# Attention followed by two expert layers on one core: a load issued by ScalarE, ten unread products, and new costs in the planner

## The chip, the core and the metric

The kernel runs on one core of a Trainium2 chip. Five engines of the core work side by side: TensorE (PE, matrix products, with its weight loads as PEld), VectorE (DVE), ScalarE (ACT), GpSimd (POOL) and SyncE (SP, which here issues the transfers). PE reads from the on-chip memory and writes sums to eight banks; the other engines read the banks and write back. The metric is the device time of one execution in microseconds (us), lower is better.

## The reference, cut to what matters

Three stages follow each other, all in float32 (the weights come as float64).

```
scores = q @ k.T / 8, causal mask, softmax       # 2 batches x 12 heads, 448 x 448, head size 64
x = (softmax @ v) laid out as 896 tokens x 768
h = x @ w_in (768 x 2048);  g = h * clip(h + 3, 0, 6) / 6;  y = g @ w_out (2048 x 768)
h = y @ w_in2;  g = P(h) / (Q(h) + 1e-6), P of degree 3, Q of degree 2;  out = g @ w_out2
```

The coefficients of P and Q come from two small arrays `a` (4 numbers) and `b` (2 numbers).

## The kernel before, in words

Every product is made to full accuracy from three products of a number's two parts (a rounded part "hi" and the rest): hi x hi, hi x rest, rest x hi.

**Attention** works on twelve pairs (two heads of one batch). For a pair, `q` and `k` are loaded by two transfers each (`qk_load`, line 340), split into hi and rest (`a_split`, line 355, and `a_rest`, line 360; for pairs 0 and 1 on ACT and DVE, later on POOL), and PE makes four row blocks of scores (`a_scores`, line 364, 24 products; the two heads sit in the two halves of PE's rows). DVE adds the mask and takes the maximum (`a_max`, line 378), ACT takes the exponential (`a_exp`, line 391), PE transposes (`a_transpose`, line 435 of the profile) into banks that ACT or DVE empties (`a_move`), and PE applies the result to `v` (`a_apply`, line 458; the two heads sit in the two halves of PE's columns). The sums of the exponentials are inverted, spread, transposed (`a_turn`, line 415) and multiplied in; `xh` and `xl` are the two parts of the result.

**The expert layers** are 2304 products of 128 x 128 weights with 448 columns (`product`, line 690). Weights come in 128 chunks of three tiles: a load (`w_load`, line 580, tile `raw`), three ACT steps (lines 592, 586, 309) and three DVE steps (596, 602, 620) turn a float64 chunk into two float32 parts. 32 chunks of the third weight stage and what follows it are made early, in the time of the first two stages: they are stored to memory (`w_keep`, line 626) and fetched when they are needed (`w_fetch`, line 630).

**The order** is written by a planner (`Program.order`, line 60). Each operation has an engine or a choice of engines, a cost, what it reads and writes, the buffers that it takes, and a due time (a place in the plan plus the number of its kind in the table `DUE`). The planner takes, again and again, the operation that can begin first by its own clock, and of those that can begin at the same time the one that is due first. What it writes down is the order on each engine; on the chip each engine runs its own list from the top and waits at each instruction for what that one needs. A load counts as 0.655 us on the queue engine (`c_dma`), and 2.2 us pass until another engine may use it. The small arrays are read by `c_load` (lines 562 and 563), turned by DVE into `cneg` (line 566) and by ACT into `cabs` (line 569).

Of the kernel before, what the change touches and what calls it, by code (L numbers as in the profile page):

```python
# [16 lines left out]
P = 128  # L17
CP = 112
NCH = 4
KC = 3  # L20
NA = 3
EARLY = 2, 3
LATE = 16
# [9 lines left out]
class Program:  # L33
# [13 lines left out]
    }  # L47
    BANKS = 8

    def __init__(self, rings, banks, due):  # L50
# [9 lines left out]
    def order(self):  # L60
        ops = self.ops
# [30 lines left out]
        def earliest(n):  # L92
            t = {}
            for e in ops[n][2]:
                t[e] = max((end[b] + self.DELAY[where[b]][e] for b in needs[n]), default=0.0)
            return t

        can = {n: earliest(n) for n in range(n_ops) if not missing[n]}
        due = [op[1] + self.due[op[0]] for op in ops]
        result = []  # L100
        while can:
            best = None
            for n, t in can.items():
# [17 lines left out]
                if room >= 1e9:  # L121
                    continue
                for e, cost in ops[n][2].items():
                    mine = max(t[e], free[e], room), due[n], n, e, cost
                    if best is None or mine < best:
                        best = mine
            if best is None:
                raise RuntimeError("no room")
            begin, _, n, e, cost = best
            start[n], end[n], where[n] = begin, begin + cost, e  # L130
            free[e] = end[n]
# [53 lines left out]
def c_dma(n):  # L185
    return n / 350e3


def c_mm(n, passes):
    return passes * n * 0.000461  # L190

# [75 lines left out]
def tile_attention_moe_moe2(  # L267
# [61 lines left out]
    def a_masks(e):  # L329
# [6 lines left out]
        )  # L336

    add("constants", -50, {"pool": 1.3}, a_masks, writes=["masks"])

    def qk_load(e, which, n):  # L340
# [133 lines left out]
    for n in range(len(pairs)):  # L474
        t = PAIR * n
        for which in ("kr", "qr"):
            raw, hl = (which, n), (SPLIT[which], n)
            add(
                "load", t, {"dma": c_dma(P * 4 * S)}, qk_load, which, n, writes=[raw],
                new=[(which, raw)],  # L480
# [11 lines left out]
        for s, (j, i) in enumerate(order):  # L492
            w = (i + 1) * CP
            if j == 0:
                sc = [("sc", n, h, i) for h in range(2)]
                add(
                    "scores", t + s, {"pe": 0.02 + c_pe(max(w, 224), 3)}, a_scores, n, i,
                    reads=[("kk", n), ("qs", n)], writes=sc, new=[("s", key) for key in sc],
                )
# [323 lines left out]
    def add_products(i, j, batches):  # L823
# [3 lines left out]
        s = [("sum", which, m, b) for b in batches]  # L827
        x = [("g", which, k, b) if which % 2 else ("x", k, b) for b in batches]
        add(
# [14 lines left out]
    for n, c in enumerate(early):  # L844
        add_chunk(c, base + 10 + (whole - 15) * n / len(early), early)
    while i < len(chunks):
# [75 lines left out]
```

## Time and profile before

| | |
|---|---|
| median of three runs | 575.91 us (575.46 to 578.22) |
| the profiled execution | 576.56 us |
| its span, first to last instruction of the program | 574.8 us |
| PE busy | 561.2 us, 98% |
| DVE busy | 440.3 us, 77% |
| ACT busy | 410.8 us, 71% |
| POOL busy | 43.8 us, 8% |
| bytes moved | 87.11 MB |

PE's products overlap and their ends are modelled, so a PE that reads as busy can still be slow or waiting; where it matters, the mean time of one instruction of a given shape and the idle time in brackets tell more than the share.

### The profile page before, as it was taken

The numbers are of one execution on the slowest core, as the hardware profiler recorded it, in microseconds if no ns is written. First come the engines' busy times: TensorE is split into PE (matmuls) and PEld (weight loads), VectorE is DVE, ScalarE is ACT, GpSimd is POOL, SyncE is SP. The second block draws the span as 40 slices with busy tenths as digits, with TensorE's granted clock in tenths as the row PEclk, the third lists the DMA queues.
The fourth block names the chain that finished last, engine by engine and source line by source line (L and its number), as shares of the span: only waits on it lengthen the run. The fifth ranks groups of instructions, "written<-read, shape, count | busy, mean of one in ns | idle before, by whom it ended". The sixth has DMA issues, their size and how long they took to land.

```text
span 574.8 us, 9134 instructions
## 1 busy us (share of the span) xinstructions
PE 561.2 (98%) x3072; PEld 496.3 (86%) x3072; DVE 440.3 (77%) x953; ACT 410.8 (71%) x925; POOL 43.8 (8%) x57
## 2 busy tenths in 40 slices
PE   5999999999999999999999999989999999999997
PEld 4666777899999999999999999979989989999996
DVE  5488888699999999876776449988988988975520
ACT  5499999797978888776676349867767767855420
POOL 3456421100000000000000000000000000000000
PEclk9999999999999999999999999999999999999999
DMA  5854112377677776776667342143322422425200
GB/s 161 233 137 123 34 33 74 105 238 261 220 235 245 227 270 230 253 259 219 217 219 247 111 137 85 56 137 114 134 84 87 160 83 83 137 89 175 87 33 32
DMA packets 35087, 87.11 MB, mean 152 GB/s; under 512 B 4512, under 2 KB 9120, under 8 KB 35040
## 3 DMA queue, kind: packets, MB, share of 16 engines
q1 hardware_dynamic: 35040, 86.53, 46.7%
q8 instruction: 24, 0.39, 0.3%
q14 instruction: 23, 0.19, 0.1%
HBM read 71.18 MB, written 15.34 MB: 151 GB/s over the span
## 4 chain that ended last, share of the span: by engine, by line
PE 73%; DVE 12%; ACT 7%; DMA 3%; issue 2%; SPq 1%; ACTq 0%
PE bank L690 60%; PE bank L435 4%; PE bank L458 4%; PE bank L373 4%; DVE p L767 2%; DVE qy L763 2%; DVE p L765 2%; DMA w<-kept 2%; ACT qy L753 1%; ACT p L735 1%; ACT qy L729 1%; DMA cb<-in_b 1%; DVE p L742 1%; DVE p L739 1%; SPq L346 1%
## 5 line engine op out<-in xcount | busy, mean ns | idle before, releaser
L690 PE MATMUL bank<-yh,w 128*128 128x448 f32 x384 | 113.3, 365 | 0.0
L690 PE MATMUL bank<-rh,w 128*128 128x448 f32 x384 | 98.7, 367 | 2.1 <-DMA w<-kept 2.0
L690 PE MATMUL bank<-xh,w 128*128 128x448 f32 x384 | 95.4, 367 | 0.0
L690 PE MATMUL bank<-ph,w 128*128 128x448 f32 x384 | 93.6, 365 | 0.0
L620 DVE TENSOR_TENSOR w<-full,w 128x384 fp32r<-128x384 f32 x96 | 53.2, 555 | 49.8 <-ACT w L309 48.8
L592 ACT ACTIVATE tail<-raw 128x384 uint32<-128x384 uint8 x128 | 70.4, 558 | 27.3 <-DVE full L596 18.0
L586 ACT ACTIVATE full<-raw 128x384 f32<-128x384 f32 x128 | 69.2, 551 | 26.1 <-DVE w L620 24.6
L596 DVE SCALAR_TENSOR_TENSOR full<-full,tail 128x384 uint32<-128x384 uint32 x128 | 70.3, 556 | 21.0 <-ACT full L586 20.3
L690 PEld LDWEIGHTS bank<-rh,w 128*128 128x128 f32 x384 | 71.7, 188 | 9.2 <-ACT qy L760 2.0
L690 PEld LDWEIGHTS bank<-yh,w 128*128 128x128 f32 x384 | 72.1, 188 | 6.0 <-DVE p L742 0.3
L690 PEld LDWEIGHTS bank<-ph,w 128*128 128x128 f32 x384 | 72.1, 188 | 5.7
L690 PEld LDWEIGHTS bank<-xh,w 128*128 128x128 f32 x384 | 71.5, 188 | 5.5
L309 ACT ACTIVATE w<-full 128x384 fp32r<-128x384 f32 x96 | 50.0, 521 | 36.4 <-PE bank L690 36.2
L690 PE MATMUL bank<-yl,w 128*128 128x448 f32 x192 | 70.1, 365 | 0.0
L602 DVE SCALAR_TENSOR_TENSOR full<-raw,full 128x384 uint32<-128x384 uint32 x128 | 68.5, 552 | 1.5
L690 PE MATMUL bank<-rl,w 128*128 128x448 f32 x192 | 55.0, 365 | 0.0
L690 PE MATMUL bank<-xl,w 128*128 128x448 f32 x192 | 54.5, 365 | 0.0
L690 PE MATMUL bank<-pl,w 128*128 128x448 f32 x192 | 54.5, 365 | 0.0
L393 ACT ACTIVATE e<-e,stat 112x448 f32<-112x448 f32 (+3 forms) x96 | 49.4, 520 | 1.2 <-DVE stat L386 1.2
L386 DVE CUSTOM_DVE_ANT_0 e<-bank,mask 112x448 f32<-112x448 f32 (+3 forms) x96 | 38.3, 442 | 7.4 <-PE bank L373 6.9
L373 PE MATMUL bank<-kk,qs 64*112 64x448 f32 (+3 forms) x288 | 33.7, 357 | 6.7 <-ACT qs L309 6.0
L690 PEld LDWEIGHTS bank<-rl,w 128*128 128x128 f32 x192 | 36.1, 188 | 2.9
(66 smaller groups left out, 774.3 us busy)
## 6 DMA issues: line engine op xcount, KB each, us to landing
raw<-in_w SPq DMA_DIRECT2D x128, 384.0 KB, 3.5
kept<-ws SPq DMA_DIRECT2D x32, 384.0 KB, 3.4
w<-kept SPq DMA_DIRECT2D x32, 384.0 KB, 3.5
kr<-in_kT SPq DMA_DIRECT2D x24, 112.0 KB, 2.8
qr<-in_qT SPq DMA_DIRECT2D x24, 112.0 KB, 2.6
v<-in_v SPq DMA_DIRECT2D x12, 224.0 KB, 2.7
out_T<-o SPq DMA_DIRECT2D x12, 224.0 KB, 3.1
ca<-in_a SPq DMA_DIRECT2D x1, 2.0 KB, 5.2
```

What stands on the lines that cost most here:

```text
L309: e.activation(out, in_, AF.Copy)
L373: e.matmul(tiles["sc", n, j, i], q[rows, qp, i * CP:w], k[rows, kp, :w], start=m == 0, stop=m == 2,)
L386: e.tensor_tensor_reduce(t[:, :w], tiles.pop(("sc", n, j, i)), mask[:, S - w:], -0.125, 3.0e38, ALU.add, ALU.min, tiles["stat", n][:, j, 0 ...
L393: e.activation(t, t, AF.Exp, bias=stat[:, j, 0, i:i + 1], scale=-1.0, accum_out=stat[:, j, 1, i:i + 1],)
L435: e.transpose(pt[:, col:col + CP], tiles["e", n, j, i][:, c * CP:(c + 1) * CP], ident)
L458: e.matmul(o[j * D:(j + 1) * D, c * CP:S], v[:, c, j * D:(j + 1) * D], segs[c, j], start=a == 0, stop=a == 2,)
L586: e.activation(full[i], high, AF.Copy, scale=TO_F32)
L592: e.activation(tail[i], top, AF.Copy, bias=-31.0 / 64.0, scale=1.0 / 32.0)
L596: e.scalar_tensor_tensor(bits, bits, 3, tail.pop(i), ALU.logical_shift_left, ALU.bitwise_or)
L602: e.scalar_tensor_tensor(bits, raw.pop(i)[:, :, :, 1], 0x80000000, bits, ALU.bitwise_and, ALU.bitwise_or)
L620: e.tensor_tensor(split[i][:, 1], full.pop(i), split[i][:, 0], ALU.subtract)
L690: e.matmul(sums[which, m, b], split[i][:, w, j, :], x, start=k == 0 and n == 0, stop=last and n == 2,)
```

## The change

Five edits. (1) The load of pair 0's `q` is given to ACT's queue instead of SP's; every `q` and `k` load counts as 1.26 us, and the delay behind a load is that of a transfer whichever engine issues it. (2) Ten products of the identity with itself, read by nobody, are put on PE ahead of the first scores; they need only the identity that POOL writes. (3) The planner knows three layouts of PE (rows split for scores, columns split for apply, whole for the rest): an operation that would change the layout counts as due 1.0 later, and a change costs PE 0.12. (4) The first products of the expert layers wait until the last pair's scores are made; a product counts as 0.000453 us a column in place of 0.000461. (5) The early chunks start 30 us later in the plan and end at the same place.

```diff
+WARM = 10
+    TILING = {"scores": "rows", "apply": "columns"}
+    DRAIN = 0.12
+    STAY = 1.0
-                t[e] = max((end[b] + self.DELAY[where[b]][e] for b in needs[n]), default=0.0)
+                t[e] = max((
+                    end[b] + self.DELAY["dma" if ops[b][0] == "load" else where[b]][e]
+                    for b in needs[n]
+                ), default=0.0)
+                turn = "pe" in t and self.TILING.get(ops[n][0], "") != tiling
                 for e, cost in ops[n][2].items():
-                    mine = max(t[e], free[e], room), due[n], n, e, cost
+                    mine = max(t[e], free[e], room), due[n] + self.STAY * turn, n, e, cost
+            if e == "pe" and self.TILING.get(ops[n][0], "") != tiling:
+                tiling = self.TILING.get(ops[n][0], "")
+                begin = max(begin, free[e] + self.DRAIN)
-    return passes * n * 0.000461
+    return passes * n * 0.000453
+    def a_warm(e, banks):
+        for _ in range(WARM):
+            e.matmul(bank[banks[0]][:CP, :CP], ident, ident, start=True, stop=True)
+    add(
+        "constants", -49, {"pe": 0.4 * WARM}, a_warm, reads=["masks"], writes=["warm"],
+        new=[("o", "warm")],
+    )
-                "load", t, {"dma": c_dma(P * 4 * S)}, qk_load, which, n, writes=[raw],
+                "load", t, {"act" if n == 0 and which == "qr" else "dma": 1.26}, qk_load, which, n, writes=[raw],
-                    reads=[("kk", n), ("qs", n)], writes=sc, new=[("s", key) for key in sc],
+                    reads=[("kk", n), ("qs", n)], writes=sc + ["scored"] * (n == len(pairs) - 1), new=[("s", key) for key in sc],
-        x = [("g", which, k, b) if which % 2 else ("x", k, b) for b in batches]
+        late = ["scored"] if which == k == 0 else []
+        x = late + [("g", which, k, b) if which % 2 else ("x", k, b) for b in batches]
-        add_chunk(c, base + 10 + (whole - 15) * n / len(early), early)
+        add_chunk(c, base + 40 + (whole - 45) * n / len(early), early)
```

The lists that the planner writes change on every engine. Three places follow. In the names, `kr`, `qr` are the loaded `k`, `q`, `kk`, `qs` their parts, the number behind them is the pair; `e1_03` is the block of pair 1, head 0, row block 3.

**The opening on ACT and DVE.** ACT before:

```order
L305 ACT_TABLE_LOAD
L309 ACTIVATE kk0_116<-kr0_101 128x448
L309 ACTIVATE qs0_122<-qr0_104 128x448
L309 ACTIVATE kk1_127<-kr1_107 128x448
L309 ACTIVATE qs1_133<-qr1_110 128x448
L393 ACTIVATE e0_03_163,stat0_162<-e0_03_163,stat0_162 112x448
```

ACT after:

```order
L318 ACT_TABLE_LOAD
L368 DMA qr0_104<-in_qT 64x448 x2
L322 ACTIVATE kk0_123<-kr0_101 128x448
L322 ACTIVATE kk1_132<-kr1_107 128x448
L322 ACTIVATE qs1_144<-qr1_120 128x448
L415 ACTIVATE e0_03_156,stat0_155<-e0_03_156,stat0_155 112x448
```

DVE before, where L362 makes a rest and L386 the maximum:

```order
L362 TENSOR_TENSOR kk0_116<-kr0_101,kk0_116 128x448
L362 TENSOR_TENSOR qs0_122<-qr0_104,qs0_122 128x448
L362 TENSOR_TENSOR kk1_127<-kr1_107,kk1_127 128x448
L362 TENSOR_TENSOR qs1_133<-qr1_110,qs1_133 128x448
L386 ISA e0_03_163,stat0_162<-bank0_71,mask_88 112x448
```

DVE after (L384 the rest, L408 the maximum):

```order
L324 CAST qs0_125<-qr0_104 128x448
L384 TENSOR_TENSOR qs0_125<-qr0_104,qs0_125 128x448
L384 TENSOR_TENSOR kk0_123<-kr0_101,kk0_123 128x448
L384 TENSOR_TENSOR kk1_132<-kr1_107,kk1_132 128x448
L408 ISA e0_03_156,stat0_155<-bank1_72,mask_88 112x448
L408 ISA stat0_155 112x1
L384 TENSOR_TENSOR qs1_144<-qr1_120,qs1_144 128x448
```

Pair 0's `q` moved from ACT's split to DVE's, and the first maximum moved ahead of the rest of pair 1's `q`.

**ACT's list around `cabs`**, the step that waits for the small array `b`. Before:

```order
L393 ACTIVATE e1_03_216,stat1_215<-e1_03_216,stat1_215 112x448
L400 ACTIVATE stat0_162<-stat0_162 112x2x4
L569 ACTIVATE cabs_92<-cb_90 128x2
L393 ACTIVATE e1_13_226,stat1_215<-e1_13_226,stat1_215 112x448
L393 ACTIVATE e1_02_243,stat1_215<-e1_02_243,stat1_215 112x336
```

After:

```order
L415 ACTIVATE e1_10_278,stat1_212<-e1_10_278,stat1_212 112x112
L415 ACTIVATE e2_03_317,stat2_316<-e2_03_317,stat2_316 112x448
L422 ACTIVATE stat1_212<-stat1_212 112x2x4
L322 ACTIVATE xh0_80<-xt0_358 128x448
L415 ACTIVATE e2_13_326,stat2_316<-e2_13_326,stat2_316 112x448
L322 ACTIVATE et1_3_397<-bank7_78 112x448
L415 ACTIVATE e2_02_336,stat2_316<-e2_02_336,stat2_316 112x336
L591 ACTIVATE cabs_92<-cb_90 128x2
L415 ACTIVATE e2_12_343,stat2_316<-e2_12_343,stat2_316 112x336
```

`cabs` moved from ahead of pair 1's second exponential to behind pair 2's third.

**SP's list in the third weight stage**, `raw` a load of weights and `w` a fetch of a chunk made early. Before:

```order
L630 DMA w76_4385<-kept76_2229 128x768
L580 DMA raw95_4455<-in_w 128x768
L580 DMA raw98_4469<-in_w 128x768
L630 DMA w78_4479<-kept78_2294 128x768
L630 DMA w79_4495<-kept79_2357 128x768
```

After:

```order
L652 DMA w76_4394<-kept76_2422 128x768
L602 DMA raw95_4470<-in_w 128x768
L652 DMA w78_4484<-kept78_2496 128x768
L602 DMA raw98_4497<-in_w 128x768
L652 DMA w79_4507<-kept79_2554 128x768
```

One weight load moved behind the fetch of chunk 78; the fetches that follow stand as before.

## Rows read from the trace of the kernel before

**Rows 1.** Busy by stage: PE, PEld, DVE, ACT, POOL (instructions), clock, DMA share, GB/s

```profile
6.00:21.70 15.70, 15.04 (x86) 11.60 (x86) 8.57 (x36) 7.73 (x24) 9.14 (x12) 1.00 0.69 188
27.50:91.90 64.40, 64.36 (x583) 44.79 (x584) 53.98 (x200) 59.67 (x196) 30.70 (x35) 1.00 0.31 83
110.70:340.00 229.30, 229.30 (x1133) 212.49 (x1132) 182.40 (x360) 171.09 (x360) 0.00 (x0) 1.00 0.67 222
```

**Rows 2.** What PE waited for in the whole span: total us, times, longest

```profile
PE bank L373 <- ACT qs L309: 6.0, 1, 6.0
PE bank L690 <- DMA w<-kept: 2.0, 2, 1.7
PE bank L435 <- ACT e L393: 1.2, 2, 0.9
```

**Rows 3.** The chain that ended last, first 34 us: start us, us, what

```profile
17.47 6.65 DMA cb<-in_b
...
27.48 1.75 PE bank L435 x16
```

**Rows 4.** ACT in order of time: start, us, instruction, idle before it

```profile
0.74 1.28 ACT L305 ACT_TABLE_LOAD   x1 [0.74 <-PEq L910]
...
4.16 0.58 ACT L309 ACTIVATE kk<-kr 128x448 fp32r<-128x448 f32 x1 [2.13 <-DMA kr<-in_kT]
5.38 0.58 ACT L309 ACTIVATE qs<-qr 128x448 fp32r<-128x448 f32 x1 [0.65 <-DMA qr<-in_qT]
6.69 0.58 ACT L309 ACTIVATE kk<-kr 128x448 fp32r<-128x448 f32 x1 [0.73 <-DMA kr<-in_kT]
...
9.87 0.67 ACT L393 ACTIVATE e<-e,stat 112x448 f32<-112x448 f32 x1 [1.24 <-DVE stat L386]
10.54 0.66 ACT L393 ACTIVATE e<-e,stat 112x448 f32<-112x448 f32 x1
...
13.70 0.55 ACT L309 ACTIVATE et<-bank 112x448 f32<-112x448 f32 x1 [0.36 <-PE bank L435]
15.45 0.54 ACT L309 ACTIVATE et<-bank 112x448 f32<-112x448 f32 x1 [0.84 <-PE bank L435]
16.20 0.54 ACT L309 ACTIVATE et<-bank 112x448 f32<-112x448 f32 x1 [0.20 <-PE bank L435]
17.01 0.66 ACT L393 ACTIVATE e<-e,stat 112x448 f32<-112x448 f32 x1
24.14 0.20 ACT L569 ACTIVATE cabs<-cb 128x2 f32<-128x2 f32 x1 [6.29 <-DMA cb<-in_b]
24.26 0.65 ACT L393 ACTIVATE e<-e,stat 112x448 f32<-112x448 f32 x1
27.70 0.66 ACT L393 ACTIVATE e<-e,stat 112x448 f32<-112x448 f32 x1
```

**Rows 5.** DVE in order of time, the last rest and the first maximum

```profile
8.67 0.63 DVE L362 TENSOR_TENSOR qs<-qr,qs 128x448 fp32r<-128x448 f32 x1 [0.75 <-ACT qs L309]
9.21 0.62 DVE L386 CUSTOM_DVE_ANT_0 e<-bank,mask 112x448 f32<-112x448 f32 x1
```

**Rows 6.** PE by shape, 6 to 23.6 us: count, busy us, mean ns

```profile
L373 PE MATMUL bank<-kk,qs 64*112 64x448 f32 x18 | 4.8, 623 | 6.7 <-ACT qs L309 6.0 <-DVE stat L386 0.6
L435 PE MATMUL bank<-ident,e 112*112 112x112 f32 x20 | 4.7, 401 | 0.0
```

**Rows 7.** The same shapes, 24 to 91 us

```profile
L373 PE MATMUL bank<-kk,qs 64*112 64x448 f32 x54 | 7.7, 388 | 0.0
L435 PE MATMUL bank<-ident,e 112*112 112x112 f32 x180 | 22.1, 265 | 1.2 <-ACT e L393 1.2
```

**Rows 8.** PE in order of time: two applies, the wait at a fetch

```profile
21.74 3.96 PE L458 MATMUL bank<-et,v 112*64 112x448 f32 x16
29.59 2.11 PE L458 MATMUL bank<-et,v 112*64 112x448 f32 x16
...
381.94 0.65 PE L690 MATMUL bank<-rh,w 128*128 128x448 f32 x2 [1.67 <-DMA w<-kept]
```

More of the change, by code (lines that the diff above doesn't have):

```diff
@@ L99, in order @@
         due = [op[1] + self.due[op[0]] for op in ops]
-        result = []
+        result, tiling = [], ""
         while can:
```

## The prediction

> **What bounds the kernel now.** I began with the busy time by stage [rows 1]. From 110.7 us on PE is the bound: 1133 products in 229.30 us are 202 ns each, without a pause. From 27.5 to 91.9 us, in attention, PE is busy for 64.36 of 64.40 us, ACT for 59.67. So whatever brings the early work forward brings the end forward, as long as ACT keeps up. Then I read what PE waited for [rows 2]: 6.0 us for the first scores, 2.0 at two fetches, 1.2 for exponentials. That is 9 us in 571, and it looks as if little were left. It is not so, because a busy PE can be slow. The same shape takes 623 ns before 23.6 us and 388 ns after it, a transpose 401 and 265 [rows 6, 7]; an apply of a whole pair takes 3.96 us at 21.7 and 2.11 at 29.6 [rows 8]. The clock column shows 1.00 for both [rows 1], so here the durations are the witness: PE runs at its lower level, 1.2 GHz, up to the first applies, and at 2.4 GHz soon after. What it did before the clock rose was scores and transposes for 15.7 us, then applies.
>
> Third, the chain of waits in the first 34 us [rows 3]. One piece of 6.65 us stands out: the load of the small array `b`. The row behind it is on ACT: `cabs` sits idle for 6.29 us, from 17.85 to 24.14 [rows 4], with pair 1's remaining seven exponentials queued behind it. PE's next large piece, sixteen transposes of pair 1, begins at 27.48 [rows 3]. From there on PE is dense to its last product. So the time is 27.48 us, plus the dense rest, and the question is how much earlier that place is reached.
>
> **The opening.** Before, the first exponential begins at 9.87 [rows 4], behind a maximum that stands in DVE's list behind the rest of pair 1's `q` (0.63 us, from 8.67 [rows 5]). After, with `q` issued by ACT at the same time as `k`, both land at about 4.16 [rows 4]. DVE then makes a cast and two rests: the cast is not in the trace at this shape; the nearest rows are 0.58 for ACT's split [rows 4] and 0.63 for a rest [rows 5], and DVE has no reason to gain or lose more than half of that; I take 0.63. That gives 4.16 + 3 x 0.63 = 6.05. Pair 1's `k` has moved up to the second place (5.38), is split by 5.96, and its rest is done at 6.68. The first bank of scores, two passes later, is there at about 7.0. Maximum 0.62, exponential at 7.7: 2.2 us earlier. The second maximum waits for the rest of pair 1's `q`, which lands third (6.69 [rows 4]): 7.62 + 0.63 + 0.62 = 8.87, its exponential at 8.95 against 10.54. So the series moves by 1.6 us.
>
> The ten products may start when the identity is written, inside ACT's table load (0.74 to 2.02 [rows 4]). They have no row; the nearest is an apply, also a product without a transpose. Its columns (448, 336, 224 and 112 for each head, the two heads side by side, so 1120 in series) take 3.96 us at the lower clock and 2.11 at the higher [rows 8], 3.5 and 1.9 ns a column, so ten products of 112 columns take 2.1 to 4.0 us and end between 3 and 6 us. The second pass of the first scores starts at 6.05, so the load's wait hides them; I take nothing, and keep half a us for the range.
>
> **The exponentials of pair 0 and 1.** Before, pair 1's first exponential begins at 17.01. In between ACT waited three times for transposes: 0.36 + 0.84 + 0.20 = 1.4 us [rows 4]. At the higher clock the transposes are a third shorter [rows 6, 7] and these waits go; at the lower they stay. I take 1.4. Then the 6.29 us at `cabs` go, because it now stands behind pair 2's third exponential, and one copy of 0.54 (as at 13.70 [rows 4]) comes in. Sum: 1.6 + 1.4 + 6.3 - 0.5 = 8.8, so PE reaches the sixteen transposes at 18.7. By then it has made six scores and four transposes fewer than before and four spread transposes more; with sixteen transposes in 1.75 us [rows 3] a group of four is 0.4 us, and the rest cancels. So 8.4 us are gained. Bounds: if PE were never held up, its work to that point, 16.7 us mostly at the lower clock and so some 8 at the higher, would end at about 14.5, a gain of 13; if the clock stays down, see below.
>
> **`cabs` in its new place.** Behind 18.7 stand on ACT a first exponential 0.65, a small step 0.2, a split 0.58, an exponential 0.65, a copy 0.54, an exponential 0.56: it is reached at 21.9. The load of `b` is still issued behind all early loads. If it lands at 24.14 as before [rows 3] ACT loses 2.2 us; with weight loads moved behind it, it may lose nothing; with the old 6.3 it would be as before. PE has an apply and scores to do meanwhile. I take 0.8.
>
> **The order on PE.** Changes of layout go from 77 to 75 in the written lists, which is nothing (two waits of tenths of a us). Before, 48 products fill PE ahead of the last apply, now 30. These 18 products, 18 x 0.202 = 3.6 us, are made later all the same, so they cost only where PE waits for the last pair's exponentials without them: 0 to 3.6 us. I take 1.0, as the list still puts 6 + 6 products between the last transposes and the last apply.
>
> **Fetches and early chunks.** PE waits 2.0 us at fetches, the longest 1.67 at 381.94 [rows 2, 8]. That fetch, of chunk 78, stood behind two weight loads and now stands behind one. I take a gain of 1.0 within 2.0 either way. The early chunks start 30 us later with the same end. DVE, which has 229.3 - 182.4 = 46.9 us free in those stages [rows 1], hides it: 30 us hold four or five of the 32 chunks, three steps of at most 0.63 each, 9 us. PE had no wait there, so nothing is to be won either.
>
> **Sum.** 576.56 us of the profiled execution (its span and 1.8 around it) - 8.4 + 0.8 + 1.0 - 1.0 = 569.0. That execution was 0.65 above the median of 575.91, so 568.3.
>
> **A rule against the load on ACT.** In the list the transfer stands behind the table load. If ACT's queue issues it only when the table is in, at 2.02 and not at 0.74 [rows 4], everything in the opening is 1.25 us later and the time is 569.6, inside the range. The Trainium skill (ScalarE: Activation LUTs, What ACT_TABLE_LOAD costs) gives a table load about 1283 ns, which this trace shows as 1.28 us, and a drain of about 1380 ns behind it, which it does not show; by that the time would be 570.9, an estimate from that page.
>
> **Rivals.** *The clock does not stay up.* What follows the ten products is paced by ACT, and PE waits between short groups of scores and transposes, the very work on which the clock stayed down before. Then PE needs 15.7 us [rows 1] from 6.0 for about the same scores and transposes, and 4 for the applies: the transposes of pair 1 begin at 25.2, the gain shrinks to 27.5 - 25.2 - 0.4 = 1.9, the new wait at `cabs` is gone, and the time is 576.56 - 1.9 + 1.0 - 1.0 - 0.65 = 574.0. If it falls only for a part of this, 571. For it: rows 6. Against: the products before the first rise were full products without a transpose, as the ten are. The Trainium skill (TensorE: Matmul & The Clock Gate, Why this matters for your kernels) warns that idle gaps between bursts of products bring the clock down again; by that rule this rival holds.
>
> *ACT becomes the bound of attention.* It is 59.67 of 64.40 busy [rows 1], with 4.7 us free in some nine pairs. If the new list loses 0.7 us a pair to exponentials that transposes wait for, ten pairs take back 7: 575.3. Against: the same steps on ACT, and PE did not wait for any in this stretch.
>
> *Slower: late fetches.* SP runs its list from the top, so a weight load that waits for DVE holds the fetch behind it. Sixteen pairs of fetches exist. If the new list makes eight come late by the present 2.0, that is 16 us: 568.3 + 1.0 + 16 = 585. It decides from the fifth (8.6 / 2.0), and shows as slower from the sixth. For it: the planner's products now count as 1.7% shorter, so its clock runs ahead of SP's waits. Against: two waits in all before, and a list that differs in one place.
>
> **How the numbers follow.** Forecast 0.60, clock 0.18, ACT 0.13, late fetches 0.09. The forecast's own range is 564.5 to 571.5: its upper side is the late load and a wait at `cabs`, its lower the gain of up to 13. To hold 8 in 10 the range takes in the clock rival: 563.5 to 574.5. A measurement of this kernel cannot tell less than 0.5%, 2.9 us, from no change. Faster by more, under 573.0: 0.59 of the forecast, 0.10 of the clock rival (its 571), 0.04 of ACT's, 0.73. Same: 0.08 and 0.08 of these two and 0.01 of the forecast, 0.17. Slower: 0.09 of the late fetches, 0.01 of ACT's, 0.10.
>
> **What would show it.** In the new profile the first exponential should begin at 7 to 8.5 us; the shape of 64 x 448 should take about 390 ns from the first scores on; sixteen transposes of pair 1 should begin near 18.7; ACT's idle time before `cabs` should be under 2.5 us; and PE should stay dense from there. The forecast is wrong if that shape still reads above 500 ns up to the first apply, if PE waits for exponentials all through attention, or if the waits for fetches exceed 4 us.

## The result, and the profile after

The kernel after took **571.8 us** in the median (566.13 to 576.74, 17 runs) beside 577.7 (574.63 to 582.55) for the kernel before in the same series: a ratio of 0.988, 95% interval 0.9853 to 0.9906. That ratio leaves out five of the 17 runs of the kernel after as slow, those more than 1.5% above its fastest; the medians of all runs give 0.990. A second series of the same two kernels gave 0.9938 (0.9903 to 0.9972). So it is faster, by some 0.6 to 1.2%. The forecast of 568.3 lies 3.5 us under the first median and 6.3 under the second one, 574.56, which is 0.06 above the range. The execution that was profiled took 575.28 us (span 573.5), in the upper part of its own spread. Why that is so turns out to be half of this case.

Busy time in the three stages of [rows 1], with the same columns:

```profile
6.00:21.70 15.70, 14.65 (x86) 11.31 (x88) 12.30 (x43) 10.07 (x32) 9.05 (x11) 1.00 0.72 196
27.50:91.90 64.40, 63.88 (x595) 44.63 (x592) 59.26 (x210) 62.97 (x208) 32.34 (x38) 1.00 0.35 108
110.70:340.00 229.30, 229.30 (x1112) 208.24 (x1111) 177.31 (x349) 167.14 (x347) 0.00 (x0) 1.00 0.66 219
```

Attention holds more work now, 595 products in place of 583, and ACT is fuller. But look at the third row: 1112 products in a stretch without a pause that held 1133 before. Each product takes longer, 206 ns in place of 202.

What PE waited for, answering [rows 2] (total, times, longest):

```profile
PE bank L354 <- POOL ident masks.py:199: 1.3, 1, 1.3
PE bank L395 <- DVE qs L324: 0.5, 1, 0.5
...
```

The 6.0 us before the first scores are covered by the ten products, nothing behind them is over 0.5, and the 2.0 us at fetches are gone from the list.

The opening on ACT, in order of time (start, us, instruction, idle before it), answering [rows 4]:

```profile
0.73 1.28 ACT L318 ACT_TABLE_LOAD   x1 [0.73 <-PEq L934]
0.76 1.46 ACTq L368 DMA_DIRECT2D qr<-in_qT  x2
5.06 0.58 ACT L322 ACTIVATE kk<-kr 128x448 fp32r<-128x448 f32 x1 [3.05 <-DMA kr<-in_kT]
...
8.94 0.67 ACT L415 ACTIVATE e<-e,stat 112x448 f32<-112x448 f32 x1 [1.44 <-DVE stat L408]
10.83 0.67 ACT L415 ACTIVATE e<-e,stat 112x448 f32<-112x448 f32 x1 [1.12 <-DVE stat L408]
...
17.15 0.66 ACT L415 ACTIVATE e<-e,stat 112x448 f32<-112x448 f32 x1
17.80 0.66 ACT L415 ACTIVATE e<-e,stat 112x448 f32<-112x448 f32 x1
...
21.72 0.55 ACT L322 ACTIVATE rs<-bank 128x448 f32<-128x448 f32 x1 [1.58 <-PE bank L437]
...
26.61 0.19 ACT L591 ACTIVATE cabs<-cb 128x2 f32<-128x2 f32 x1
```

Three readings. ACT's queue issued the load of `q` inside the table load, at 0.76. Pair 1's second exponential follows its first at once (17.80 against 24.26 before), and `cabs` finds its data there, with no idle time at all. And pair 1's first exponential begins at 17.15, where it began at 17.01 before: the opening brought nothing forward.

The same stretch on DVE and on POOL (two views, of the kernel after):

```profile
5.39 0.39 DVE L324 CAST qs<-qr 128x448 fp32r<-128x448 f32 x1 [5.39 <-DMA qr<-in_qT]
...
8.82 1.43 DVE L384 TENSOR_TENSOR qs<-qr,qs 128x448 fp32r<-128x448 f32 x1
```

```profile
8.63 1.14 POOL L384 TENSOR_TENSOR kk<-kr,kk 128x448 fp32r<-128x448 f32 x1
9.71 0.96 POOL L324 CAST qs<-qr 128x448 fp32r<-128x448 f32 x1
10.62 0.56 POOL L324 CAST kk<-kr 128x448 fp32r<-128x448 f32 x1
```

The rest that took 0.63 us in [rows 5] takes 1.43 beside a POOL that works on tiles of the same size, and POOL's own cast takes 0.96 there and 0.56 a little later. In the two runs below in which SP issues the load, POOL begins at 9.20, behind the start of that rest, and the rest takes 0.62 again.

PE by shape from 6 to 20.2 us, where [rows 6] stood (count, busy us, mean ns), and PE in order of time:

```profile
L395 PE MATMUL bank<-kk,qs 64*112 64x448 f32 x18 | 5.4, 637 | 1.3 <-DVE qs L324 0.5 <-DVE stat L408 0.4 <-DVE kk L384 0.4
L457 PE MATMUL bank<-ident,e 112*112 112x112 f32 x20 | 4.5, 400 | 0.0
```

```profile
1.33 4.08 PE L354 MATMUL bank<-ident 112*112 112x112 f32 x20 [1.33 <-POOL ident masks.py:199]
5.93 0.71 PE L395 MATMUL bank<-kk,qs 64*112 64x448 f32 x2 [0.52 <-DVE qs L324]
...
21.61 2.11 PE L480 MATMUL bank<-et,v 112*64 112x448 f32 x16
23.65 1.75 PE L457 MATMUL bank<-ident,e 112*112 112x112 f32 x16
...
102.94 0.55 PE L437 MATMUL bank<-ident,rb 112*128 112x112 f32 x4
```

Ten products, which the trace lists as twenty, take 4.08 us and end 0.52 before the scores can begin. In this execution they did not bring the clock up: the shapes read 637 and 400 ns, as before, so this is the 1.2 GHz level until shortly before the first applies. Pair 1's transposes begin at 23.65, not at the forecast 18.7, and not at 27.48.

**Where the time went, closed to the last tenth.** Call the distance from the start of one expert product to the start of the next the pitch. In the mean over a stretch it is either 202.7 or 206.7 ns, never in between, and it holds for 40 products to over 1300. From each trace I took four quantities: the end of attention on PE, the number of expert products ahead of it, the number of products behind it at each of the two pitches, and what is left of the gaps (a gap or pause below is a distance from product to product that is longer than the pitch). Attention ends on PE with four small products that turn the spread sums (`a_turn`, at 102.94 in the fence above); they follow the last apply, after 17 expert products in the kernel after. Below, "end of attention" is the end of these four.

| | before | after |
|---|---|---|
| attention ends | 110.75 us, behind 48 products | 103.48 us, behind 30 |
| 18 products x 0.2027 made later | | +3.65 |
| products at the higher pitch | 0 of 2255 | 1344 of 2273 |
| lost in gaps beyond the pitch | 3.28 | 0.24 |

So: -7.27 + 3.65 by the end of attention is -3.62 us; the gaps give -3.04; 1344 products x 4.0 ns take +5.38. The sum is -1.28, and 576.56 - 575.28 is 1.28. The profiled execution of the kernel before had no product at the higher pitch, that of the kernel after had 59% of them there. Counted with all at 202.7 ns the two would have taken 576.56 and 569.90.

### The profile page after: what moved, and what is told of

Its sections match the earlier page's. It is cut to its first block, busy times and chain, and to the rows that moved or that the text cites. A ratio compares the mean times of both kernels' runs of the same rounds, so it can differ in the third digit from the quotient of the medians.

```text
span 573.5 us, 9140 instructions
## 1 busy us (share of the span) xinstructions
PE 566.3 (99%) x3092; PEld 499.3 (87%) x3092; DVE 446.2 (78%) x955; ACT 412.9 (72%) x920; POOL 47.4 (8%) x60
## 4 chain that ended last, share of the span: by engine, by line
PE 95%; DVE 3%; DMA 1%; issue 0%; ACT 0%; SPq 0%; DVEq 0%
PE bank L712 82%; PE bank L457 4%; PE bank L480 4%; PE bank L395 4%; DVE e L408 1%; PE bank L437 1%; DMA kr<-in_kT 1%; DVE et L324 0%; SPq L368 0%; DVE full L618 0%; DVE full L624 0%; DVE qs L384 0%; DVE rb L324 0%; DVE xt L448 0%; DVE w L642 0%
## 5 line engine op out<-in xcount | busy, mean ns | idle before, releaser
L712 PE MATMUL bank<-ph,w 128*128 128x448 f32 x384 | 95.0, 368 | 0.0
L608 ACT ACTIVATE full<-raw 128x384 f32<-128x384 f32 x128 | 69.1, 551 | 23.2 <-DVE w L642 22.2
L624 DVE SCALAR_TENSOR_TENSOR full<-raw,full 128x384 uint32<-128x384 uint32 x128 | 70.5, 566 | 1.6
L408 DVE CUSTOM_DVE_ANT_0 e<-bank,mask 112x448 f32<-112x448 f32 (+3 forms) x96 | 38.6, 440 | 5.9 <-PE bank L395 5.5
L712 PEld LDWEIGHTS bank<-pl,w 128*128 128x128 f32 x192 | 36.0, 188 | 3.7
L712 PEld LDWEIGHTS bank<-xl,w 128*128 128x128 f32 x192 | 36.0, 188 | 3.7
```

The source lines that it names most:

```text
L408: e.tensor_tensor_reduce(t[:, :w], tiles.pop(("sc", n, j, i)), mask[:, S - w:], -0.125, 3.0e38, ALU.add, ALU.min, tiles["stat", n][:, j, 0 ...
L608: e.activation(full[i], high, AF.Copy, scale=TO_F32)
L624: e.scalar_tensor_tensor(bits, raw.pop(i)[:, :, :, 1], 0x80000000, bits, ALU.bitwise_and, ALU.bitwise_or)
L712: e.matmul(sums[which, m, b], split[i][:, w, j, :], x, start=k == 0 and n == 0, stop=last and n == 2,)
```

## The experiments

Two questions were open. The first: which edit earns the 3.6 us, and why not 8.4? The theory is that the end of the stall at `cabs` earns it, and that PE's lower clock keeps the rest back; the rivals are the load on ACT's queue and the ten products. The second: what sets the two pitches, the written list, or does PE take one anew where it is held up?

**The kernel after, again.**

> The changed kernel once more, for a second profile. In the first one the products between 105 and 340 us take 206.7 ns each, against 202.7 in the kernel before; that is 1137 x 4.0 ns = 4.5 us. Theory 'state': the pitch belongs to one execution and not to the list, so a run near 566 to 567 us shows 202.7 there and PE's wait for fetches still gone. Theory 'list': the pitch comes with the new lists (other banks, other chunks beside it), so it is 206.7 in every profile, and the time is 571 to 572.

Median 574.56 (572.18 to 578.15) beside 577.51. Its profile differs from the first where it matters. PE by shape from 11.1 to 20 us, columns as above, and PE in order of time:

```profile
L457 PE MATMUL bank<-ident,e 112*112 112x112 f32 x20 | 2.8, 269 | 0.0
L395 PE MATMUL bank<-kk,qs 64*112 64x448 f32 x11 | 1.8, 416 | 0.0
```

```profile
17.61 0.57 PE L437 MATMUL bank<-ident,rb 112*128 112x112 f32 x4 [0.55 <-ACT e L415]
18.11 2.11 PE L480 MATMUL bank<-et,v 112*64 112x448 f32 x16
20.15 1.75 PE L457 MATMUL bank<-ident,e 112*112 112x112 f32 x16
```

The same list, with the clock's step to 2.4 GHz at 11.0 us in place of 20.2: the shapes read 269 and 416 ns, pair 1's transposes begin at 20.15, attention ends at 100.01. Here the change is worth 107.10 - 100.01 = 7.1 us at the end of attention (the kernel before counted at 30 products, 110.75 - 3.65), near the 8.4 - 0.8 - 1.0 of the forecast. Yet the execution took 572.18, because 1296 products ran at the higher pitch, 5.2 us. That the higher pitch came back here, from the end of attention to 368 us, spoke for the list as what sets it.

**Without the ten products**, and the same twice more:

```diff
-        for _ in range(WARM):
+        for _ in range(0):
```

> The changed kernel without the ten unread products, every list else the same. Theory 'products raise the clock': in the changed kernel the shape of 64 x 448 goes to its short time at about 20 us and not at 23.6, and without the products it is late again; the applies of pair 0 then take nearly 4 us in place of 2.1, and the time is 2 to 4 us longer. Theory 'products idle': the step in the clock stays at 20 us, the opening keeps its times within 0.3 us, and the time is the same within 1 us.

> The kernel after without its ten products, a second execution under the profile. Products bring the step forward: it comes at 20 us or later again (20.33 the first time), and pair 1's sixteen transposes begin at 23.4 to 23.8. Chance: in this and the next run together one step comes before 15 us, as it did in two of three profiles with the products.

> The kernel after without its ten products, a third execution under the profile. Products bring the step forward: 20 us or later. Chance: one of this and the run ahead of it steps before 15 us. For the products' pitch (202.7 or 206.7 ns): if the list sets it, the switches come at the same places as in the first execution; if it is drawn where PE is held up, at others.

The median tells little: 576.21, a ratio of 0.9951 (0.9921 to 0.9982), inside the interval that the kernel after itself gave in the same series. The profiles tell more. The clock's step came at 20.3, 22.8 and 22.0 us, so none of the three came before 15 us. Attention ended at 103.46, 104.29 and 103.95, with pair 1's transposes at 23.61, 24.41 and 24.10; the second of these is later than expected. The products went down to the lower pitch at 371.6, 372.4 and 372.0 us, always at the same place of the list, which again spoke for the list. A row of the third one, 6 to 21 us:

```profile
L395 PE MATMUL bank<-kk,qs 64*112 64x448 f32 x18 | 5.4, 637 | 6.7 <-DVE qs L324 6.0 <-DVE kk L384 0.4 <-DVE stat L408 0.3
```

**The kernel after, a third time under the profile.**

> The kernel after, unchanged, a third execution under the profile. Products bring the step forward more often than not: a step at 10 to 14 us with transposes of pair 1 at about 20.2, or, as in the first profile, 20 us and 23.7. The time is worked out from the share of products at each of the two pitches: about 566 with all at 202.7 ns and an early step, 575 at 206.7, 3.5 more with a late step; a time off this by more than 1 us speaks against the two pitches as what spreads the executions.

An early step, at 14.5 us; transposes of pair 1 at 21.42, the end of attention at 101.31; 1296 products at the higher pitch. The expectation's own figures give 566 + 5.2 = 571.2; measured were 572.92, off by 1.7, so its test failed as it was put. What was off is the rough 566: the run with SP's issue below has an early step and no product at the higher pitch, and took 568.15. From that one, 568.15 + 5.18 is 573.3, which is 0.4 from the measured time; but this was worked out afterwards.

**`cabs` alone, in the kernel before.** Both small steps are emitted behind the first split of `xh`; nothing else changes.

```diff
+        late = [x for x in plan if x[0][3].__name__ in ("c_neg", "c_abs")]
+        plan = [x for x in plan if x[0][3].__name__ not in ("c_neg", "c_abs")]
+        at = [x[0][3].__name__ for x in plan].index("a_hi") + 1
+        plan[at:at] = late
```

> The kernel before, with nothing changed but that the two steps on the small arrays (cneg on DVE, cabs on ACT) stand behind the first result of pair 0. Theory of the prediction (the 6.3 us in which ACT waited at cabs were on the path): the sixteen transposes of pair 1 begin near 21 us in place of 27.5 and the time is 6 us shorter. Rival (PE at its lower clock was nearly as late by itself: its apply of pair 0 ran from 21.7 to 25.7): they begin near 25.5, and the time is 1.5 to 2.5 us shorter.

573.88 in the median of six, a ratio of 0.9892 (0.9845 to 0.9939): as much as the whole change in its first series, and no less than the 0.9938 of the whole change in this same series. ACT and PE of this run, in order of time:

```profile
16.93 0.66 ACT L398 ACTIVATE e<-e,stat 112x448 f32<-112x448 f32 x1
17.59 0.20 ACT L405 ACTIVATE stat<-stat 112x8 f32<-112x8 f32 x1
17.68 0.66 ACT L398 ACTIVATE e<-e,stat 112x448 f32<-112x448 f32 x1
...
24.94 0.54 ACT L314 ACTIVATE et<-bank 112x448 f32<-112x448 f32 x1 [2.97 <-PE bank L440]
```

```profile
21.67 2.33 PE L463 MATMUL bank<-et,v 112*64 112x448 f32 x16
23.93 2.13 PE L440 MATMUL bank<-ident,e 112*112 112x112 f32 x20
```

The stall of 6.29 us is gone, the second exponential is 6.6 us earlier, but PE reaches the transposes only 3.55 us earlier and ACT now waits 2.97 for PE. The wait changed its owner: with PE at the lower clock, PE's own work ends at 23.9. That lies between the two theories, 21 and 25.5. Attention ends 107.1 - 103.9 = 3.2 us earlier by this move alone, of the 3.6 of the whole change. Both are good to about 1 us only: the same early list ended attention at 107.1 and at 106.0 in two executions.

**`cabs` back, in the kernel after**: the same edit the other way, behind pair 1's first exponential, with SP's list unchanged.

```diff
+        at = [x[0][3].__name__ == "a_exp" and x[0][4][0] == 1 for x in plan].index(True) + 1
+        to = [x[0][3].__name__ for x in plan].index("c_load") + 1
+        loads = [x for x in plan[at:to] if x[1] == "dma"]
+        plan[at:to] = loads + late + [x for x in plan[at:to] if x[1] != "dma"]
```

> The kernel after with one part undone: cabs stands again behind pair 1's first exponential on ACT, where it stood before; the transfers keep their order. The array b lands near 24.8 us, as in the kernel after. Theory A, that the move of cabs is nearly all that the change gains by the end of attention: ACT sits idle 5 to 7 us before cabs, pair 1's second exponential begins near 25, its sixteen transposes at 27 to 28.5, the last apply ends 3 to 5 us later than in the kernel after (106.5 to 108.5 with 30 products ahead of it, in place of 100 to 103.5), and the median is that of the kernel before within 0.4%. Theory B, that the opening and the ten products carry it, ACT catching up behind the stall: the last apply ends within 1.5 us of the kernel after's, and the median is that of the kernel after.

581.25, a ratio of 1.0043 (1.0004 to 1.0081): no faster than the kernel before, though all else of the change is still in. The times below are a little later than theory A had. The profiled execution, 575.93, is one of the shortest of the ten and has no product at the higher pitch; what the others lose beyond it has no profile. ACT, then PE, then two stretches (columns of [rows 1]):

```profile
14.43 0.66 ACT L422 ACTIVATE e<-e,stat 112x448 f32<-112x448 f32 x1
23.45 0.20 ACT L598 ACTIVATE cabs<-cb 128x2 f32<-128x2 f32 x1 [8.27 <-DMA cb<-in_b]
23.56 0.65 ACT L422 ACTIVATE e<-e,stat 112x448 f32<-112x448 f32 x1
```

```profile
24.23 0.98 PE L444 MATMUL bank<-ident,rb 112*128 112x112 f32 x4 [8.32 <-DVE rb L331]
25.14 4.00 PE L487 MATMUL bank<-et,v 112*64 112x448 f32 x16
29.08 1.75 PE L464 MATMUL bank<-ident,e 112*112 112x112 f32 x16
```

```profile
6.00:18.00 12.00, 8.64 (x80) 6.27 (x80) 8.62 (x37) 7.42 (x24) 8.79 (x11) 1.00 0.65 187
20.00:29.00 9.00, 4.76 (x20) 2.28 (x20) 3.17 (x12) 4.82 (x19) 0.00 (x0) 0.50 0.37 89
```

The clock had come up at 5.2 us. Then ACT stood 8.27 us at `cabs`, PE 8.32 us behind it, and the granted clock fell to 0.50: an apply of a pair takes 4.00 us again, where it took 2.11. Attention ends at 108.93. So an early step is given back by one long wait. The Trainium skill (TensorE: Matmul & The Clock Gate, Why this matters for your kernels) warns of that, and this trace agrees, with 0.50 behind a pause of 8.32 us.

**The load issued by SP instead of ACT**, the rest of the kernel after as it is:

```diff
-            e.dma_start(tiles[which, n][j * D:(j + 1) * D], src)
+            nc.sync.dma_start(tiles[which, n][j * D:(j + 1) * D], src)
```

> The changed kernel with pair 0's q issued by SP again, between pair 0's and pair 1's k; plan and all else as in the changed kernel. Theory 'parallel issue wins': the first exponential begins 0.6 us or more later than 8.94, and the second, which waits for pair 1's q, later than 10.83 by up to 1.3; the time grows by 1 us. Theory 'it only shares the same transfers': pair 0's k lands at 4.2 again and not at 5.06, so the first exponential moves by less than 0.5 us and the time by less than 0.7.

572.85 (568.15 to 578.38), 0.9879 (0.9831 to 0.9926): no loss. `k` now lands earlier and the first exponential is where it was:

```profile
4.26 0.58 ACT L322 ACTIVATE kk<-kr 128x448 fp32r<-128x448 f32 x1 [2.25 <-DMA kr<-in_kT]
...
9.05 0.67 ACT L415 ACTIVATE e<-e,stat 112x448 f32<-112x448 f32 x1 [0.48 <-DVE stat L408]
...
10.13 0.67 ACT L415 ACTIVATE e<-e,stat 112x448 f32<-112x448 f32 x1 [0.32 <-DVE stat L408]
```

With two issuers `k` reached ACT at 5.06 and 5.39 in two profiles of the kernel after, with SP alone at 4.26; `q` reached DVE at 5.39 and 5.68 there and at 5.50 here. So ACT's queue does not bring `q` forward and puts `k` back by 0.8 to 1.1 us. The second exponential, at 10.13, is 0.7 us earlier without it (10.83 in the first profile): this edit cost the opening a little.

**Fourteen products and SP's issue**, to leave PE no pause ahead of the scores:

```diff
-        for _ in range(WARM):
+        for _ in range(14):
```

> The kernel after with two edits: SP issues pair 0's q as well, and 14 unread products in place of ten; the planner's lists are otherwise those of the kernel after. Ten products took 4.08 us from 1.33 in the kernel after, so 14 take about 5.7 and end near 7.0, close to where the second pass of the first scores begins (7.04). Theory A, that the unread products bring PE's step to 2.4 GHz forward whenever they leave no pause ahead of the scores: the shape 64 x 448 reads about 400 ns from 8 us on, the step comes at 8 to 14 us, pair 1's sixteen transposes begin at 19.5 to 20.5, the last apply ends at 99.5 to 101.5, and the median lies 2 to 4 us under that of the kernel after, about 569. Theory B, that the step's time is chance from execution to execution: the profile shows a step anywhere from 10 to 24 us, and the median is that of the kernel after, 572 to 575.

The profile is nearly theory A's, the median is theory B's. The step came at 7.5 us and attention ended at 101.00, but PE waited 1.95 us for a load of `v` in between, and pair 1's transposes began at 21.16. The median, 574.33 (568.51 to 579.55; ratio 0.9948, 0.9920 to 0.9976), misses the expected 569. Between all products at one pitch and all at the other lie 9 us; that the median fell to the unlucky side here is not shown, since only the profiled execution has its pitches on record.

**PE held up ahead of single sums**, in the kernel after: two unread products of 64 x 64 ahead of a sum, with POOL rewriting the tile between them.

```diff
+        if k == 0 and m % 3 == 0 and 0 in batches:
+            o = bank[banks[0]][:64, S:512]
+            for _ in range(2):
+                nc.gpsimd.memset(pause, 0.0)
+                e.matmul(o, pause, pause, start=True, stop=True)
```

> The kernel after with PE held up on purpose, ahead of sixteen or more sums of the expert layers: PE makes an unread product of 64 x 64, POOL rewrites the tile that it read, PE makes a second one from it. Each hold costs PE 0.5 to 1.5 us. Theory A, that the pitch of the products (202.7 or 206.7 ns) is drawn anew where PE is held up: between two holds the pitch is constant, it switches at some of the holds and nowhere else, and both values show between 110 and 360 us. Theory B, that the pitch belongs to the execution and to a place near 370 us, where it has switched in most profiles of this list: no switch ahead of 360 us whatever the holds.

One hold on PE, and four stretches between holds with the expert products alone (window, length, PE busy and count, PEld, clock, DMA share, GB/s):

```profile
162.54 0.33 PE L711 MATMUL bank<-pause 64*64 64x64 f32 x2
163.13 0.33 PE L711 MATMUL bank<-pause 64*64 64x64 f32 x2 [0.26 <-POOL pause L710]
163.38 0.68 PE L718 MATMUL bank<-xh,w 128*128 128x448 f32 x2
```

```profile
120.00:139.00 19.00, 19.00 (x96) 17.60 (x95) 1.00 0.56 193
165.00:185.00 20.00, 20.00 (x99) 18.16 (x98) 1.00 0.65 220
220.00:276.00 56.00, 56.00 (x278) 51.90 (x277) 1.00 0.71 243
279.00:336.00 57.00, 57.00 (x277) 51.78 (x276) 1.00 0.59 199
```

56 us hold one product more than 57. From start to start the pitch is 202.6, 206.6, 202.7 and 206.7 ns in these four. Of 18 stretches of over 30 products between pauses of PE, six are at the higher value and twelve at the lower, and none changes inside. Between the end of attention and 360 us, where the six other profiles of this list show no switch, there are five here, each at a hold. So a hold can fix the pitch anew, and it then keeps: theory A.

Three things limit this. The four small products at the end of attention do the same without a pause: in all seven profiles of this list the expert products ahead of them run at the lower value and those behind them at the higher. Two changes stand at no pause at all: one at 381.7 us of the first profile of the kernel after, at distances of 204, 209, 211 and 196 ns, and one at 423.9 of the run with the fetch alone, where nothing shows but a distance of 198 ns. And it is not pure chance: the six other profiles, three of them without the ten products, all ran at 206.7 up to a pause near 370 us (0.33 us from one product to the next), where five went down and one, the first of the kernel after, only 9 us later. What in PE decides for one or the other is not shown. Nor is it settled whether the change itself makes the higher value more likely: the three profiles with the order of before ran at 202.7 to at least 376 us, eight of eleven with the new lists at 206.7 from the end of attention on. (This run's 585.79 us is the price of the holds.)

**The fetch alone, in the kernel before**: chunk 78 fetched ahead of the weight load.

```diff
+        load, fetch = names.index(("w_load", (98,))), names.index(("w_fetch", (78,)))
+        plan.insert(load, plan.pop(fetch))
```

> The kernel before with one move on SP's list: the fetch of chunk 78 stands ahead of the weight load that stood before it, as in the kernel after. Theory A, that this place alone made the waits at fetches go: the gap of 2.04 us at 381.94 is gone, the gaps near 426 and 470 (0.43 and 0.71 together 1.1) stay, and PE loses 1.0 to 1.8 us between the last apply and its end beyond what the pitches give, against 3.28 in the kernel before. Theory B, that the wait only moves to the next fetch or that the other gaps go with it: a gap over 1 us at another fetch, or under 0.5 in all.

What PE waited for at fetches:

```profile
PE bank L694 <- DMA w<-kept: 0.2, 1, 0.2
```

The gap of 2.04 us at 381.94 is gone. Gaps of 0.56, 0.50 and 0.50 us stand at 379.4, 468.3 and 490.6; beyond the pitches PE loses 1.52 in place of 3.28 us. So this place is worth 1.8 us, and the loss is the one of theory A; the gap near 426, which it had as staying, went too, and small ones came at 379 and 491.

**Layouts and early chunks undone, in the kernel after:**

```diff
-    DRAIN = 0.12
-    STAY = 1.0
+    DRAIN = 0.0
+    STAY = 0.0
-        add_chunk(c, base + 40 + (whole - 45) * n / len(early), early)
+        add_chunk(c, base + 10 + (whole - 15) * n / len(early), early)
```

> The kernel after with two edits undone in the planner: changes of layout cost and delay nothing, and the early chunks start 30 us earlier as before. The lists then hold 77 changes of layout, as before, and more products ahead of the last apply. The prediction took both edits at nothing apart from those products: counted at 30 products, at 0.203 us each, the last apply ends at 100 to 101.5 with an early step of the clock or at 103 to 104.5 with a late one, and PE loses under 1 us beyond the pitches behind it. The other theory: the layouts carry a part of the gain, and the last apply ends at 105 or later, so counted.

Attention ends at 106.26 behind 42 products, so at 103.83 counted at 30; 0.64 us are lost beyond the pitches. In this one execution neither edit carries a part of the gain that can be seen. The clock is worth a look, though (6 to 12 and 13 to 19 us, columns of [rows 1], then a row of PE in order of time):

```profile
6.00:12.00 6.00, 3.71 (x35) 2.84 (x36) 5.63 (x15) 3.15 (x9) 3.38 (x5) 1.00 0.62 181
13.00:19.00 6.00, 6.00 (x34) 4.79 (x34) 3.97 (x19) 5.05 (x18) 2.37 (x4) 0.50 0.77 234
```

```profile
10.75 1.57 PE L395 MATMUL bank<-kk,qs 64*112 64x448 f32 x11 [1.49 <-DVE stat L408]
```

It came up at 5.7 us, fell at 12.6, after PE had stood for 1.49 us at 9.26 waiting for a maximum, and came back at 19.4.

**All profiles side by side.** Step: where the trace first shows 2.4 GHz. End: end of attention on PE, counted at 30 products ahead of it. Higher pitch: products at 206.7 ns. The last column is the profiled time less 4.0 ns for each product at the higher pitch.

| kernel | step | end | higher pitch | time | at 202.7 ns |
|---|---|---|---|---|---|
| before | 23.7 | 107.1 | 0 | 576.56 | 576.6 |
| before, fetch alone | 21.4 | 106.0 | 216 | 574.54 | 573.7 |
| before, `cabs` alone | 22.2 | 103.9 | 599 | 574.56 | 572.2 |
| after | 20.2 | 103.5 | 1344 | 575.28 | 569.9 |
| after, again | 11.0 | 100.0 | 1296 | 572.18 | 567.0 |
| after, third | 14.5 | 101.3 | 1296 | 572.92 | 567.7 |
| SP issues | 13.3 | 101.4 | 0 | 568.15 | 568.2 |
| SP, fourteen | 7.5 | 101.0 | 929 | 571.53 | 567.8 |
| no products | 20.3 | 103.5 | 1296 | 575.78 | 570.6 |
| no products, second | 22.8 | 104.3 | 1296 | 576.31 | 571.1 |
| no products, third | 22.0 | 104.0 | 1296 | 575.93 | 570.7 |
| layouts, chunks undone | 5.7, fell | 103.8 | 1284 | 575.76 | 570.6 |
| `cabs` back | 5.2, fell | 108.9 | 0 | 575.93 | 575.9 |

With unread products the first step came before 15 us in seven of eight profiles (that with the holds, 10.8, is not in the table), without them in none of six. Where it came early and stayed, attention ended at 100.0 to 101.4, and in the kernel after without the products at 103.5 to 104.3: they are worth some 3 us, in most of the profiled executions and not in all. At one pitch throughout, the three profiles of the kernel after lie 6.7, 9.6 and 8.8 us under that of the kernel before.

## Why the prediction was right, and where it was not

**The place and the direction were right.** The chain's stall at `cabs` was the thing to remove. Moving it alone gives 0.9892, and with it put back nothing of the gain is left. But by the signs that the prediction set itself its mechanism failed in the first profile: 64 x 448 read 637 ns up to the first apply, where over 500 was to count against it, the first exponential came at 8.94 in place of 7 to 8.5, and pair 1's transposes at 23.65 in place of 18.7.

**The opening was mis-sized.** "That gives 4.16 + 3 x 0.63 = 6.05 ... exponential at 7.7", with 8.95 for the second and 1.6 us won. Measured: 8.94 and 10.83, the second 0.29 later than before. Two reasons show. The landing time of 4.16 was taken from a trace in which SP alone issued; with ACT issuing beside it, it became 5.06 for `k` and 5.39 for `q`. And the rest of 0.63 us became 1.43 with POOL beside it. DVE's cast was 0.39, not 0.63. The load on ACT's queue earned nothing.

**Ten products, hidden: right.** They took 4.08 us (2.1 to 4.0 said) and ended at 5.41, ahead of the first scores. Their cost hides in the load's wait, as forecast; what they bring, an earlier step of the clock, was not a term of its own.

**A rule against the load on ACT: it did not hold here.** The issue is at 0.76, 0.03 us behind the table load's start, so the transfer paid neither for the load nor for anything behind it. Of the drain that the Trainium skill (ScalarE: Activation LUTs, What ACT_TABLE_LOAD costs) sets behind a load this trace cannot tell, as ACT's next step is only at 5.06.

**The series of exponentials: ACT's sum was not the limit.** "So PE reaches the sixteen transposes at 18.7" is the step that failed. The stall went (8.4 to be gained, of it 6.3 here), but that sum is ACT's alone, and at the lower clock PE's work ends later: 23.65, a gain of 3.8. In the same list with an early clock it is 20.15, a gain of 7.3. The forecast took the clock as up from the first scores on, and named the other case a rival with 25.2 for this place (its terms, 6.0 + 15.7 + 4, add to 25.7). The first profile is that rival, about 2 us milder, and with another cause: the clock did not fall back, it did not come up before 20.2. That it can come up and fall back, the run with `cabs` back and the one with the layouts undone show. The bound "16.7 us mostly at the lower clock" stood in the text and should have been made into a sum: 6.0 + 16.7 alone gives a floor near 23.

**`cabs` in its new place, 0.8: nothing.** The array was there when ACT came, at 26.6 and at 23.1 with an early clock.

**The end of attention, 1.0: about 0.2.** What the transposes gained, 3.8, arrives at the end of attention as 3.6. PE had no wait over 0.5 us there, though ACT was 62.97 of 64.40 us busy; the rival in which ACT becomes the bound did not come.

**Fetches, -1.0 within 2.0 either way: -3.0 in the first profile,** between -2.3 and -3.0 in the others of the same list without holds. The moved place alone is -1.8. The rival of late fetches was wrong: PE lists no wait for one.

**What was missing is the pitch.** It takes 9.1 us (2273 x 4.0 ns) from an execution or leaves it, and neither text nor range had it. The time came near all the same. At the lower pitch throughout, the three profiles of the kernel after give 569.9, 567.0 and 567.7 against the 569.0 worked out for the profiled execution: with an early clock the mechanism pays about what was forecast, with a late one the gaps, at -3.0 in place of -1.0, made up for two of the three us that the end of attention missed (3.6 in place of 6.6). That the median of executions with unknown shares of the two pitches and of early and late clocks then fell 3.5 us from the forecast is in part luck; the second series, at 574.56, fell 6.3 from it. "202 ns each, without a pause" in [rows 1] is one of two values, and the trace of before had only shown one.

## What to carry to other kernels

When a stall on one engine is to go, add up the other engine's work to the same place at the speed that it has there: the later of the two sums sets the gain. Split two executions into the end of a stage, counts, pauses and the mean distance of the steady instruction before their times are compared; a steady stretch that runs 2% slower hides a change of 1%. A small step that waits for a small late load belongs where the load has landed, whatever the place it was due at.

## What the runs showed of the hardware

- The same dense products, 128 x 128 by 448, run at 202.7 or 206.7 ns each. In the slower case every distance is 206 or 207 ns in the first profile of the kernel after (205 to 208 in the second); in the faster one they vary from 199 to 207. Most changes of the value stand where PE is held up or makes four small products of another shape, two stand at no pause (381.7 us of the kernel after, 423.9 of the fetch alone). At the pause near 371 one execution of the kernel after kept the higher value and two left it.
- The clock's step to 2.4 GHz came at 5.2 to 20.2 us in executions whose PE works from 1.33 us on, and it fell again, to 0.50 in the record, in two of these eight (during a pause of PE of 8.32 us in the one, after one of 1.49 in the other). Before its first step the record reads 1.00 at shapes that run at nearly half speed (64 x 448 at 637 ns in the first profile of the kernel after, and at 384 from 21 us on).
- A small array of 1 KB took 6.65 us to land in the kernel before [rows 3], where SP issued two weight loads right behind it, and 3.4 us in the kernel after, where the next one was issued 3.9 us behind it.
- With SP and ACT both issuing, pair 0's `k` reached ACT at 5.06 us (5.39 in the second profile), with SP alone at 4.26; `q` gained nothing by it.
- A difference of two 128 x 448 tiles on DVE took 1.43 us while POOL worked on tiles of that size, and 0.62 us where POOL began behind it.
